# Fused linear attention and gated MLP on one core: the first chunk's k and r scaled on one engine, and two of four small norm steps of five chunks moved to another

## The chip, the cores and the metric

The kernel runs on one core of a Trainium2 chip. The metric is the device time of one execution in microseconds, the median of several runs; lower is better. The engines are named as in the profile: PE is the matrix engine (PEld its weight loads), DVE is VectorE, ACT is ScalarE, POOL is GpSimd, and SP is the queue that issues the transfers. Each works through its own list of instructions in order, and waits on the others through semaphores.

## The reference

Two stages follow one another. The first is a linear attention with a decaying state, over 4 batches, 8 heads, 768 steps and 48 channels per head:

```python
for t in range(S):
    cur = einsum('bhd,bhe->bhde', u * kt, vt)
    y[:, :, t] = einsum('bhd,bhde->bhe', rt, state + cur)
    state = w * state + einsum('bhd,bhe->bhde', kt, vt)
```

The second is a gated MLP on its output `x` (4 x 768 x 384):

```python
h = maximum(x @ w_in, 0)             # 1024 columns: u is the first half, v the second
v_n = (v - mean(v)) / sqrt(var(v) + 1e-6)
v_s = einsum('ts,bsd->btd', w_spatial, v_n) + b_spatial
out = (u * v_s) @ w_out
```

All of it is in float32; the large products are made of three passes over high and low parts of the operands.

## The kernel before, in words

The attention is done in 24 chunks of 128 time steps, 6 for each batch. For a chunk, `prep` (L588) multiplies k and r by powers of the decay (step "scale", L605), forms the products r·k·u (steps "rk", L609, and "rku", L610; for the first chunk "prod", L620, summed on PE, L627), scales another copy of k (step "ks", L615), sums (step "red", L632) and spreads the sums on a diagonal (step "dia", L635). `g1` (PE, L652 and L660) makes the scores and the state updates, `mid` masks and copies (L683 to L697), and `g2` (PE, L714) gives the chunk's part of `x`, which is split into high and low parts (steps "xh" on ACT and "xl" on DVE, L755).

For each chunk of x, `moe_v` (L768) then computes v (PE, L762 to L764) and normalizes it along the row. For the first five chunks ("early", `STA = 5`, all in batch 0) the row's sum and its sum of squares come from accumulating activations on ACT (L786, L790). Then follow, on columns of 128x1: the step "sqrt" on ACT (L797), the step "scales" on DVE, which is four instructions (L803 to L806), and the step "norm" on ACT (L815, L816). Columns of the small tile `q` are called `at(n)`: `at(7)` is the sum of squares, `at(9)` the root, and `at(12)` the factor that the norm multiplies by. The four steps of "scales" are one Newton step on the root and a reciprocal:

```python
e.tensor_scalar(out=p8(), in0=at(7), scalar1=part, scalar2=0.25 * EPS, op0=ALU.mult, op1=ALU.add)
e.reciprocal(out=at(10), in_=at(9))
e.tensor_scalar(out=p11(), in0=p8(), scalar1=at(10), scalar2=at(9), op0=ALU.mult, op1=ALU.add)
e.reciprocal(out=at(12), in_=p11())
```

In batch 0 the two intermediate columns `p8` and `p11` lie in PSUM (tile `cc`).

Two other steps matter below. `part` (L536) splits a loaded tile `wst` of the spatial weights into a high part on ACT and a low part on POOL (step "ws lo", L539); the 4 places of `wst` are taken again by the next loads when the low part is done. `from_f64` (L490) converts the other weights from double precision, mostly on DVE.

The order is not left to a scheduler of the compiler. A planner (`Plan`, L86) knows each step with the engines that it may run on and an estimated duration for each, simulates the engines, and chooses engine and start for every step. `issue` (L314) then writes the instructions in the order of the planned starts, and so fixes each engine's list. In that order, around the norms of the five early chunks, POOL's list and the DVE step that stands behind each "scales" are as follows ("sqrt" and "scales" mark only the places of these steps of ACT and DVE):

| chunk | POOL's list with the places of sqrt and scales | DVE's next step behind scales |
|---|---|---|
| 0 | rku, (sqrt 0), ws lo, (scales 0), rk, dia | red |
| 1 | rku, (sqrt 1), ws lo, ws lo, dia, rk, ws lo, (scales 1), rku, ws lo | first xl |
| 2 and 3 | (sqrt 2), rk, (sqrt 3), rku, (scales 2), ws lo, ws lo, ws lo, (scales 3), dia | 2: scale of k; 3: scale of r |
| 4 | dia, (sqrt 4), ab lo, (scales 4), ws lo, ws lo | red |

In the first chunk the planner put the scale of k on POOL and that of r on DVE, to start together; each reads two tiles in SBUF. "ab lo" (L825) is the low part of a normalized block of v.

Of the kernel before, what the change touches and what calls it, by code (L numbers as in the profile page):

```python
# [10 lines left out]
AF = mybir.ActivationFunctionType  # L11
ALU = mybir.AluOpType
# [14 lines left out]
ND = DH // P  # L27
TH = S // 2
EPS = 1e-6
GAIN, SHUN, HOLD = 2.0, 2.0, 40.0  # L30
SEEDS = ()
FIRST = """
# [53 lines left out]
class Plan:  # L86
# [6 lines left out]
    def op(self, eng, f, r=(), w=(), psum=(), dma=0, name="", after=(), port=None, n=0):  # L93
        o = Op()
        o.i, o.eng, o.f, o.preds, o.succ, o.bufs, o.new, o.dma = len(self.ops), eng, f, set(), [], [], [], dma
        o.n = n
        o.name, o.on, o.port = name, None, "P" in eng if port is None else port
        o.lag = 0.165 if "E" in eng else 0.0
        for x, write in [(x, False) for x in r] + [(x, True) for x in w] + [(x, True) for x in psum]:
            b, sub = x if isinstance(x, tuple) else (x, None)  # L100
            if o not in b.ops:
                if not b.ops and b.group:
                    o.new.append(b)
                b.ops.append(o)
                o.bufs.append(b)
            subs = list(b.state) if sub is None else [sub, None]
            for s in subs:
                if s in b.state:
                    last, readers = b.state[s]
                    if last is not None:  # L110
                        o.preds.add(last)
                    if write:
                        o.preds.update(readers)
            if write:
                if sub is None:
                    b.state = {None: (o, [])}
                else:
                    b.state[sub] = (o, [])
            else:
                for s in (list(b.state) if sub is None else [sub]):  # L120
                    b.state.setdefault(s, (b.state.get(None, (None, []))[0], []))[1].append(o)
                if sub is None and None not in b.state:
                    b.state[None] = (None, [o])
        o.preds.update(after)
        o.preds.discard(o)
        self.ops.append(o)
        return o
# [55 lines left out]
    def repeat(self, t0, seeds):  # L183
# [6 lines left out]
        if seeds:  # L190
            x, y = (sum(z) for z in zip(*(self.change(s) for s in seeds)))
            T = self.run(t0, x, y)
        return T

# [112 lines left out]
    def take(self, b, t):  # L307
# [3 lines left out]
        d.free.remove(x)  # L311
        b.slot = x[1]

    def issue(self, engines):  # L314
        for o in sorted(self.ops, key=lambda o: (o.start, o.i)):
            for b in o.new:
                b.tile = b.group.pool.tile(b.shape, b.dt, name=b.name, tag=b.slot, bufs=1)
            o.f(engines[o.on])


@with_exitstack
def fused_kernel(ctx, tc, rkT, rN, kN, vN, wT, uB, w_in, w_sp, b_sp, w_out, out):
    nc = tc.nc
# [6 lines left out]
    plan = Plan()  # L330
    op = plan.op
# [18 lines left out]
    def act(n):  # L350
        return (n + 185) / 1200
# [42 lines left out]
    eps = fixed([P, 1], "eps")  # L394
# [10 lines left out]
    q = lambda: tmp()[:, 0:256].rearrange("p (n c) -> p n c", n=NP)  # L405
# [32 lines left out]
    def raw_sp(s, t, i):  # L438
# [5 lines left out]
       name="warm")  # L444
# [5 lines left out]
    for p in range(NP):  # L450
        op({"V": 0.25}, lambda e, p=p: e.tensor_tensor_scan(
            out=q()[:, p, :], data0=wt()[:, p:p + 1].to_broadcast([P, 64]), data1=zz(), initial=1.0, op0=ALU.mult, op1=ALU.add),
           r=[wu, (tmp, "z")], w=[(tmp, "q", )], name="scan")
# [3 lines left out]
       w=[w128], name="w128")  # L457
    op({"P": 0.1}, lambda e: e.memset(uw(), 0.0), w=[(uw, j) for j in range(2)], name="memset")
    for j in range(2):
        op({"P": 0.25}, lambda e, j=j: e.tensor_tensor(  # L460
            out=uw()[64 * j:64 * j + 64, :, j], in0=wu()[64 * j:64 * j + 64, NP:2 * NP], in1=wu()[64 * j:64 * j + 64, 0:NP],
            op=ALU.mult), r=[wu], w=[(uw, j)], name="uw")
    op({"P": 0.3}, lambda e: e.tensor_tensor(out=diag(), in0=eye()[:, 0:64], in1=eye()[:, 64:P], op=ALU.add), r=[eye], w=[diag],
       name="diag")
    op({"P": 0.15}, lambda e: e.memset(mask(), 1.0), w=[mask], name="memset")
    for o, sign in ((64, 1), (0, -1)):
        op({"P": 0.3}, lambda e, sign=sign, o=o: e.affine_select(
            out=mask()[o:o + 64], in_=mask()[o:o + 64], pattern=[[-sign, 64]], compare_op=ALU.is_gt, fill=0.0, base=0,
# [299 lines left out]
    def moe_v(b, c):  # L768
        xh, xl = xs_all[b, c // 3]
        i, h = c % 3, c // 3  # L770
        o = slice(i * C, (i + 1) * C)
        pm = Buf(gM, [P, 512], F32, "pm")
        assert b * NC + c in there

        def f(e):
            for j in range(NK):
                mm3(e, pm(), xh()[:, j, o], xl()[:, j, o], wi[0][0]()[:, j], wi[0][1]()[:, j], j == 0, j == NK - 1)

        op({"E": 2.09}, f, n=18, r=[(x, (i, z)) for x in (xh, xl) for z in range(2 if b * NC + c < XPM else 1)] + wi[0], psum=[pm], name="v")
        if i == 0:  # L780
            vt[b, h] = Buf(gV, [P, 3, DH], F32, "v")
        vf, q = vt[b, h], Buf(gSM, [P, 16], F32, "q")
        at = lambda k: q()[:, k:k + 1]
        early = b * NC + c < STA
        if early:
            op({"A": act(DH) + 0.16}, lambda e: e.activation(out=vf()[:, i], in_=pm(), func=AF.Relu, accum_out=at(0)),  # L786
               w=[(vf, i), (q, 0)], psum=[pm], name="v")
            op({"A": 0.2}, lambda e: e.mul(at(6), at(0), -1.0 / DH), r=[(q, 0)], w=[(q, 6)], name="mean")
            junk = Buf(gF, [P, DH], mybir.dt.bfloat16, "junk", "j", 1)
            op({"A": sb(DH) + 0.3}, lambda e: e.activation(out=junk(), in_=vf()[:, i], func=AF.Square, bias=at(6), accum_out=at(7)),  # L790
               r=[(vf, i), (q, 6)], w=[junk, (q, 7)], name="square")
        else:
            acopy((vf, i), lambda: vf()[:, i], pm, lambda: pm(), DH, True, "v", {"V": vec(DH)}, AF.Relu)
            op({"V": 0.69}, lambda e: e.bn_stats(out=q()[:, 0:6], in_=vf()[:, i]), r=[(vf, i)], w=[(q, 0)], name="stats")
            op({"V": 0.18}, lambda e: e.bn_aggr(out=q()[:, 6:8], in_=q()[:, 0:6]), r=[(q, 0)], w=[(q, 6), (q, 7)], name="aggr")
        part = 0.25 / DH if early else 0.25
        op({"A": 0.2}, lambda e: e.activation(out=at(9), in_=at(7), func=AF.Sqrt, bias=eps(), scale=part), r=[(q, 7), eps],  # L797
           w=[(q, 9)], name="sqrt")
        o8 = DM + HC + 2 * ((b * NC + c) % 8)
        p8, p11 = (lambda: at(8), lambda: at(11)) if b else (lambda: cp()[:, o8:o8 + 1], lambda: cp()[:, o8 + 1:o8 + 2])  # L800

        def scales(e):
            e.tensor_scalar(out=p8(), in0=at(7), scalar1=part, scalar2=0.25 * EPS, op0=ALU.mult, op1=ALU.add)  # L803
            e.reciprocal(out=at(10), in_=at(9))
            e.tensor_scalar(out=p11(), in0=p8(), scalar1=at(10), scalar2=at(9), op0=ALU.mult, op1=ALU.add)
            e.reciprocal(out=at(12), in_=p11())  # L806
            if not early:
                e.tensor_scalar(out=at(13), in0=at(6), scalar1=at(12), scalar2=-1.0, op0=ALU.mult, op1=ALU.mult)  # L808

        op({"V": 0.65 if early else 0.81}, scales, r=[(q, 6), (q, 7), (q, 9)], w=[(q, 10)] + ([] if b else [(cc, ("q", o8))]), name="scales", port=not early)  # L810

        def norm(e):
            x = vf()[:, i]
            if early:
                e.mul(at(13), at(6), at(12))  # L815
            e.activation(out=x, in_=x, func=AF.Identity, bias=at(13), scale=at(12))  # L816

        op({"A": 1.01 if early else 0.81}, norm, r=[(q, 10), (q, 6)], w=[(vf, i)], name="norm")
# [81 lines left out]
    def late(b, t, d):  # L900
        pm = Buf(gM, [P, 512], F32, "pm")
        xh, xl = xs_all[b, t]
        x = xsum[b, t, d]
        assert {b * NC + 3 * t + x for x in range(3)} <= there
        uv = lambda: pm()[:, 0:TH]

        def f(e):
            for j in range(NK):
                mm3(e, uv(), wi[1][0]()[:, j, blk[d]], wi[1][1]()[:, j, blk[d]], xh()[:, j], xl()[:, j], j == 0, j == NK - 1)

        op({"E": 1.6}, f, n=18, r=[xh, xl, *wi[1]], psum=[pm], name="u")
        op({"V": vec(TH)}, lambda e: e.scalar_tensor_tensor(out=uv(), in0=uv(), scalar=0.0, in1=x(), op0=ALU.max, op1=ALU.mult),  # L912
           r=[x], psum=[pm], name="gate")
        gt = gs[b, t, d] = Buf(gAB, [P, 2, TH], F32R, "gt")
        acopy((gt, 0), lambda: gt()[:, 0], pm, uv, TH, True, "gt hi")
        op({"V": vec(TH)}, lambda e: e.tensor_tensor(out=gt()[:, 1], in0=uv(), in1=gt()[:, 0].bitcast(F32), op=ALU.subtract),
           r=[(gt, 0)], w=[(gt, 1)], psum=[pm], name="gt lo")
# [157 lines left out]
    for b in range(B):  # L1075
# [3 lines left out]
        o = [(lambda b=b, t=t, i=i: moe_out(b, t, i)) for t in range(2) for i in range(3)]  # L1079
        dr = [lambda b=b: (s3(b), direct(b, 0))]  # L1080
        if b:
# [4 lines left out]
            A = [Step(m) for m in range(6 * b, 6 * b + 10)]  # L1086
# [13 lines left out]
    for f in seq:  # L1100
        f()
    T = plan.repeat(14.0, SEEDS)
    plan.issue({"E": nc.tensor, "A": nc.scalar, "V": nc.vector, "P": nc.gpsimd, "S": nc.sync})


# [53 lines left out]
```

## Time and profile before

| what | value |
|---|---|
| median of 3 runs | 345.95 us (344.8 to 346.01) |
| profiled execution, its own time | 346.39 us |
| span in its profile | 344.7 us |
| busy: PE, DVE, ACT, POOL | 326.5, 258.0, 155.9, 198.1 us |
| PE instructions (matmuls) | 5414 |
| data moved | 43.87 MB in 26263 packets |

The span is the time from the first to the last instruction of the profiled execution; about 1.7 us lie around it. Starts in the rows are counted from the start of the span. A row of the timeline has the start, the duration, the engine, the line of the kernel, the operation, the tiles it writes and reads, and in brackets the time for which the engine was idle before it and what ended that. A row of the chain of waits has the start, the duration and the work that the end of the program is traced back to at that time. A row of the stretches has, for each engine, its busy time and (x) its instructions within that stretch.

### The profile page before, as it was taken

The page shows a single profiled execution, that of the slowest core. Times are in us where ns is not written, and L with a number is a line of the kernel's source. Part 1 is how long each engine was busy: PE and PEld are TensorE (multiplying, and loading weights), DVE is VectorE, ACT ScalarE, POOL GpSimd, SP SyncE. Part 2 cuts the span into 40 slices and gives each one's busy share as a digit, 9 for nine tenths or more (in the row PEclk, how much of TensorE's full clock was granted, in tenths as well). Part 3 has the DMA queues.
Part 4 walks back from the last instruction along what each step waited for, and adds up shares of the span by engine and source line. Part 5 has one row for each costly group of instructions (what it writes and reads, how often), then busy time and mean ns, then how long its engine had stood idle before and what let it go on. Part 6 is the DMA issues. An engine that isn't in the chain of part 4 may idle for free.

```text
span 344.7 us, 12648 instructions
## 1 busy us (share of the span) xinstructions
PE 326.5 (95%) x5414; PEld 297.5 (86%) x5414; DVE 258.0 (75%) x567; ACT 155.9 (45%) x372; POOL 198.1 (57%) x193
## 2 busy tenths in 40 slices
PE   2887798999999999999999999999999999999996
PEld 2665687899999898999899888999998799999995
DVE  6897799898989878899887688688476575674520
ACT  5433899832453547614413555623043546331121
POOL 5767586654799969989955154989052020840000
PEclk9999999999999999999999999999999999999999
DMA  7989588653513735514423253414041000100012
GB/s 235 387 235 327 169 256 298 199 174 114 193 60 104 226 120 164 172 39 142 139 63 104 74 175 103 151 60 142 0 126 55 28 25 34 59 0 0 3 46 91
DMA packets 26263, 43.87 MB, mean 127 GB/s; under 512 B 3040, under 2 KB 15328, under 8 KB 26208
## 3 DMA queue, kind: packets, MB, share of 16 engines
q1 hardware_dynamic: 26208, 43.07, 39.2%
q8 instruction: 42, 0.69, 0.9%
q14 instruction: 13, 0.11, 0.1%
HBM read 38.34 MB, written 4.72 MB: 125 GB/s over the span
## 4 chain that ended last, share of the span: by engine, by line
PE 83%; DMA 4%; POOL 4%; issue 3%; DVE 2%; ACT 2%; SPq 1%; DVEq 0%; POOLq 0%
PE pm L945 20%; PE pm L762 16%; PE pm L764 15%; PE pm L763 15%; PE xp L714 8%; PE ps L652 4%; PE ps L660 3%; DMA wst<-w_sp 2%; DMA kn<-kN 1%; POOL ws L539 1%; PE pm L714 1%; PE pm L520 1%; SPq L363 1%; POOL rn L609 1%; POOL rn L610 1%
## 5 line engine op out<-in xcount | busy, mean ns | idle before, releaser
L945 PE MATMUL pm<-wst,ab 128*128 128x384 f32 x216 | 41.2, 339 | 0.5 <-issue 0.5
L376 ACT CAST gt<-pm 128x384 fp32r<-128x384 f32 x26 | 12.4, 480 | 60.4 <-DVE pm L912 57.6
L825 POOL TENSOR_TENSOR ab<-v,ab 128x384 fp32r<-128x384 f32 x22 | 23.8, 1093 | 26.4 <-ACT ab L376 26.4
L945 PEld LDWEIGHTS pm<-wst,ab 128*128 128x128 f32 x216 | 37.7, 188 | 0.8 <-issue 0.6
L762 PE MATMUL pm<-xh,wiuh 128*128 128x384 f32 x96 | 32.9, 343 | 0.0
L762 PE MATMUL pm<-woh,gt 128*128 128x384 f32 x96 | 32.9, 343 | 0.0
L764 PE MATMUL pm<-woh,gt 128*128 128x384 f32 x96 | 32.5, 338 | 0.3 <-issue 0.3
L764 PE MATMUL pm<-xh,wiul 128*128 128x384 f32 x96 | 32.4, 337 | 0.0
L763 PE MATMUL pm<-wol,gt 128*128 128x384 f32 x96 | 32.3, 337 | 0.0
L763 PE MATMUL pm<-xl,wiuh 128*128 128x384 f32 x96 | 32.3, 337 | 0.0
L945 PE MATMUL pm<-ws,ab 128*128 128x384 f32 x162 | 31.5, 338 | 0.0
L635 POOL TENSOR_TENSOR a<-diag,dg 128x512 f32<-128x512 f32 x17 | 17.9, 1053 | 23.1 <-PE xp L714 8.9
L762 PE MATMUL pm<-wivh,xh 128*128 128x512 f32 x72 | 29.2, 406 | 1.0 <-ACT wiuh L376 1.0
L376 ACT COPY sb<-t 64x192 f32<-64x192 f32 x48 | 16.8, 350 | 27.3 <-DVE t L690 26.7
L945 PEld LDWEIGHTS pm<-ws,ab 128*128 128x128 f32 x162 | 28.6, 188 | 0.1
L764 PE MATMUL pm<-wivh,xl 128*128 128x512 f32 x72 | 28.5, 396 | 0.0
L763 PE MATMUL pm<-wivl,xh 128*128 128x512 f32 x72 | 28.5, 395 | 0.0
L609 POOL TENSOR_TENSOR rn<-rn,kn 128x384 f32<-128x384 f32 x16 | 17.5, 1091 | 15.1 <-DMA kn<-kN 8.2
L610 POOL TENSOR_TENSOR rn<-rn,ub 128x384 f32<-128x384 f32 x21 | 23.2, 1106 | 4.9 <-DVE rn L609 3.8
L957 DVE TENSOR_TENSOR tp<-pm,tp 128x384 f32<-128x384 f32 x30 | 16.6, 553 | 10.4 <-PE pm L945 10.1
L816 ACT ACTIVATE v<-v,q 128x512 f32<-128x512 f32 x24 | 19.5, 815 | 7.5 <-DVE q L808 7.1
L683 DVE COPY_PREDICATED a<-mask,ps 128x512 f32<-128x512 uint32 x24 | 17.8, 742 | 6.5 <-PE ps L660 6.3
(169 smaller groups left out, 876.4 us busy)
## 6 DMA issues: line engine op xcount, KB each, us to landing
kT<-rkT SPq DMA_DIRECT2D x24, 256.0 KB, 3.7
rT<-rkT SPq DMA_DIRECT2D x24, 256.0 KB, 3.5
vn<-vN SPq DMA_DIRECT2D x24, 256.0 KB, 4.1
kn<-kN SPq DMA_DIRECT2D x24, 200.0 KB, 3.4
wst<-w_sp SPq DMA_DIRECT2D x24, 192.0 KB, 4.2
out<-ob SPq DMA_DIRECT2D x24, 192.0 KB, 1.9
rn<-rN SPq DMA_DIRECT2D x23, 192.0 KB, 3.0
raw<-w_in SPq DMA_DIRECT2D x8, 384.0 KB, 5.1
```

The costliest lines, as they stand in the source:

```text
L376: e.activation(out=o_f(), in_=i_f(), func=func) if func else e.copy(o_f(), i_f())
L609: op(VP, lambda e: e.tensor_tensor(out=rn()[:, 0:DM], in0=rn()[:, 0:DM], in1=kn()[:, 0:DM], op=ALU.mult), r=[kn], w=[rn], name="rk")
L610: op(VP, lambda e: e.tensor_tensor(out=rn()[:, 0:DM], in0=rn()[:, 0:DM], in1=ub(), op=ALU.mult), r=[ub], w=[rn], name="rku")
L635: op({"V": vec(512) + 0.05, "P": 1.06}, lambda e: e.tensor_tensor(out=a().rearrange("s j p t -> s (j p) t"), in0=(diagp() if e is nc.vecto ...
L683: op({"V": 0.74}, lambda e: e.copy_predicated(out=a(), mask=mask().bitcast(U32).unsqueeze(1).unsqueeze(1).to_broadcast([P, 2, NP, HC]), da ...
L714: e.matmul(x[z][32 * g:32 * g + 32, jt * HC:(jt + 1) * HC], lhsT, rhs, start=(z, g) not in began, stop=True, skip_group_check=True, tile_p ...
L762: e.matmul(o, lh, rh, start=first, stop=False)
L763: e.matmul(o, lh, rl, start=False, stop=False)
L764: e.matmul(o, ll, rh, start=False, stop=last)
L816: e.activation(out=x, in_=x, func=AF.Identity, bias=at(13), scale=at(12))
L825: op(VP, lambda e: e.tensor_tensor(out=t()[:, 1], in0=src(), in1=t()[:, 0].bitcast(F32), op=ALU.subtract), r=[(t, 0), src_b], w=[(t, 1)], ...
L945: e.matmul(pm(), a()[:, x, i], w()[:, y, i], start=not began and i + q_ == 0, stop=i + q_ == 4, skip_group_check=True)
```

## The change

The step "sqrt" of an early chunk now also issues, on POOL, the first of the four scale steps (`at(8)` from `at(7)`). "scales" issues the first reciprocal on DVE, then the second `tensor_scalar` (`at(11)`) on POOL, and hands the last reciprocal to `issue`, which writes it on DVE right behind the next DVE step, or ahead of the first step that depends on "scales", whichever comes first. The intermediate columns lie in the SBUF tile `q`. The planner knows nothing of it: its costs and its order are the same. After planning, every "scale" step that was planned to start before 7 us is put on DVE; these are k and r of the first chunk, of which r was there already. `DEBUG` is never set.

```diff
+    rest = None
     def issue(self, engines):
+        left = None
         for o in sorted(self.ops, key=lambda o: (o.start, o.i)):
 ...
+            if self.rest and left in o.preds:
+                self.rest()
+                self.rest = None
+            late = self.rest
             o.f(engines[o.on])
+            if late and o.on == "V":
+                late()
+                self.rest = None if self.rest is late else self.rest
+            if self.rest and self.rest is not late:
+                left = o
 ...
-        op({"A": 0.2}, lambda e: e.activation(out=at(9), in_=at(7), func=AF.Sqrt, bias=eps(), scale=part), r=[(q, 7), eps],
-           w=[(q, 9)], name="sqrt")
+        def root(e):
+            e.activation(out=at(9), in_=at(7), func=AF.Sqrt, bias=eps(), scale=part)
+            if early:
+                nc.gpsimd.tensor_scalar(out=at(8), in0=at(7), scalar1=part, scalar2=0.25 * EPS, op0=ALU.mult, op1=ALU.add)
+        op({"A": 0.2}, root, r=[(q, 7), eps], w=[(q, 9)], name="sqrt")
 ...
         def scales(e):
+            if early:
+                e.reciprocal(out=at(10), in_=at(9))
+                nc.gpsimd.tensor_scalar(out=at(11), in0=at(8), scalar1=at(10), scalar2=at(9), op0=ALU.mult, op1=ALU.add)
+                plan.rest = lambda: e.reciprocal(out=at(12), in_=at(11))
+                return
 ...
     T = plan.repeat(14.0, SEEDS)
+    for o in plan.ops:
+        if o.name == "scale" and o.start < 7:
+            o.on = "V"
     plan.issue({"E": nc.tensor, "A": nc.scalar, "V": nc.vector, "P": nc.gpsimd, "S": nc.sync})
```

More of the change, by code (lines that the diff above doesn't have):

```diff
@@ L29 @@
 EPS = 1e-6
+DEBUG = None
 GAIN, SHUN, HOLD = 2.0, 2.0, 40.0
@@ L1102, in fused_kernel @@
     T = plan.repeat(14.0, SEEDS)
+    if DEBUG:
+        DEBUG(plan, T)
+    for o in plan.ops:
+        if o.name == "scale" and o.start < 7:
+            o.on = "V"
     plan.issue({"E": nc.tensor, "A": nc.scalar, "V": nc.vector, "P": nc.gpsimd, "S": nc.sync})
```

## The prediction

> **What bounds the kernel now.** I read the busy times at the head of the page first, then the table of stretches, then what PE waited for, and only then the timeline where the edited steps stand.
>
> ```profile
> PE 326.5 (95%) x5414; PEld 297.5 (86%) x5414; DVE 258.0 (75%) x567; ACT 155.9 (45%) x372; POOL 198.1 (57%) x193
> ...
> 36.00:46.00 10.00, 9.20 (x206) 7.22 (x206) 8.78 (x23) 8.48 (x25) 5.97 (x7) 1.00 0.62 174
> 46.00:56.00 10.00, 9.18 (x293) 7.23 (x291) 9.58 (x27) 9.11 (x28) 7.21 (x8) 1.00 0.86 276
> 56.00:66.00 10.00, 9.84 (x110) 9.15 (x111) 8.89 (x28) 8.83 (x23) 6.67 (x7) 1.00 0.82 262
> 66.00:80.00 14.00, 13.83 (x320) 12.59 (x318) 12.80 (x25) 6.55 (x17) 8.66 (x9) 1.00 0.46 148
> 80.00:120.00 40.00, 40.00 (x743) 36.53 (x740) 35.61 (x74) 19.22 (x45) 33.74 (x34) 1.00 0.47 142
> ```
>
> PE (the number behind each stretch's length) is full from about 68 us on. So what delays PE before that is not made good later: a shift there arrives at the end almost whole. Before 68 us PE has gaps, and DVE in the stretch from 46 to 56 is busy for 9.58 of 10 us. All edits stand before 65 us. What PE waited for in that time is this (us in total, times, longest):
>
> ```profile
> PE pm L714 <- issue: 2.8, 2, 2.0
> PE ps L660 <- issue: 2.2, 2, 1.2
> PE pm L762 <- ACT wiuh L376: 1.0, 1, 1.0
> PE ps L652 <- DVE rT L605: 0.9, 1, 0.9
> PE xp L714 <- ACT sb L376: 0.2, 1, 0.2
> ```
>
> The largest, 2.8 and 2.2 us, are ascribed to no engine ("issue"), so no edit of POOL or DVE reaches them. The 0.9 us before L652 is the first chunk's scale, which is edited. The last row, 0.2 us, is the last gap before PE is full: there ACT, not PE, sets the pace.
>
> **The first chunk's scales.** One DVE step is added, one POOL step removed.
>
> ```profile
> 5.27 1.27 POOL L605 TENSOR_TENSOR kT<-kT,tt 128x512 f32<-128x512 f32 x1 [1.43 <-DVE w L456]
> 5.33 1.75 DVE L605 TENSOR_TENSOR rT<-rT,tt 128x512 f32<-128x512 f32 x1 [0.19 <-DVE w L456]
> ...
> 6.79 0.59 ACT L1019 COPY cc<-tt 128x512 f32<-128x512 f32 x1
> 7.20 0.98 PEld L652 LDWEIGHTS ps<-rT,kT 64*64 64x64 f32 x32 [1.24 <-POOL kT L605]
> ...
> 7.42 0.55 DVE L615 TENSOR_TENSOR kn<-kn,cc 128x384 f32<-128x384 f32 x1 [0.33 <-ACT cc L1019]
> ...
> 8.04 0.98 PEld L660 LDWEIGHTS ps<-vn,kn 64*64 64x64 f32 x32
> ...
> L601 DVE TENSOR_TENSOR kT<-kT,tt x8: 692/1094/1383, 114.0 to 256.5; 128x512 f32<-128x512 f32 x8
> ```
>
> Beside POOL's scale, DVE's took 1.75 us and ended at 7.08. The same operation on the same kind of tiles has a minimum of 0.69 us (last row, min/median/max); I take that, since POOL then has nothing to run until its "prod" step, which itself needs both scales. Two of them on DVE end at 5.33 + 2 x 0.69 = 6.71, 0.37 us sooner, and L652 starts so much sooner. But PE's next group, L660, needs kn from L615. That started at 7.42, with DVE free since 7.08, because it waited for ACT's L1019 (6.79 + 0.59 = 7.38), which the edit does not touch. So kn is still ready at 7.42 + 0.55 = 7.97, and L660's weights were loaded from 8.04. The sooner start ends in a gap between L652 and L660. I take 0; the end of the range is a gain of 0.4 us, if L615's wait is put down to the wrong step.
>
> **The norm's steps, what is saved.** Per early chunk DVE loses the two `tensor_scalar` steps.
>
> ```profile
> 53.60 1.01 POOL L609 TENSOR_TENSOR rn<-rn,kn 128x384 f32<-128x384 f32 x1 [2.70 <-DMA kn<-kN]
> ...
> 54.43 0.15 DVE L803 TENSOR_SCALAR cc<-q 128x1 f32<-128x1 f32 x1
> ...
> 54.68 0.28 DVE L805 TENSOR_SCALAR cc<-cc,q 128x1 f32<-128x1 f32 x1
> 54.69 1.00 POOL L610 TENSOR_TENSOR rn<-rn,ub 128x384 f32<-128x384 f32 x1
> 54.99 0.17 DVE L806 RECIPROCAL q<-cc 128x1 f32<-128x1 f32 x1
> 55.08 0.67 DVE L605 TENSOR_TENSOR kT<-kT,cc 128x512 f32<-128x512 f32 x1
> 55.65 3.01 POOL L539 TENSOR_TENSOR ws<-wst,ws 128x384 fp32r<-128x384 f32 x3
> 55.66 0.61 DVE L755 TENSOR_TENSOR xl<-pm,xh 128x192 fp32r<-128x192 f32 x2
> ...
> 56.47 0.19 PEld L764 LDWEIGHTS pm<-wivh,xl 128*128 128x128 f32 x1
> ...
> 56.68 1.31 SPq L363 DMA_DIRECT2D wst<-w_sp  x2
> ```
>
> The four steps take 55.08 - 54.43 = 0.65 us of DVE. Two reciprocals remain, like L806 0.17 us each, so 0.31 us are saved per chunk, 1.6 us over five. That is worth something only where DVE is what PE waits for, and none of PE's waits above names a DVE step but L605 of the first chunk. I count the saving at nothing.
>
> **The norm's steps, what is added.** Each chunk adds two POOL steps of one column, and DVE's last reciprocal now waits for POOL with all of DVE queued behind it. The nearest rows for such a POOL step are the smallest ones it runs:
>
> ```profile
> L460 POOL TENSOR_TENSOR uw<-wu x2: 196/230/263, 2.5 to 2.7; 64x4 f32<-64x4 f32 x2
> ```
>
> No row has a POOL `tensor_scalar`. On DVE, the second one (with two columns as scalars) took 0.28 against 0.15 us for the first. I take 0.25 us for each of the two POOL steps, nearest to L460; the ends are 0.1 (part hidden behind the step before) and 1.0 us (the full POOL step of L610, 128x384). The Trainium skill, in "GPSIMD Engine Reference", section 4.1 "Engine selection", advises VectorE for elementwise work because GpSimd is about twice as slow on two-input operations. By that rule, twice DVE's 0.15 and 0.28 us would give 0.86 us for the pair instead of my 0.5, an estimate; no row here decides it.
>
> Where it counts is decided by the order of POOL's list. I go through the chunks with what covered POOL:
>
> ```profile
> POOL ws L539 <- ACT ws L376: 3.7, 2, 3.3
> POOL rn L609 <- DMA kn<-kN: 3.4, 2, 2.7
> POOL ab L825 <- ACT ab L376: 3.4, 2, 1.7
> ...
> POOL wst L539 <- ACT wst L376: 1.3, 1, 1.3
> ```
>
> - Chunk 0: the first step falls into the 3.3 us wait before "ws lo". The second delays "rk" and "rku" by 0.25 us, and the 1.3 us wait before the next "ws lo" takes that up. Cost 0.
> - Chunk 1: the first step falls into that 1.3 us. The second pushes "rku" and a "ws lo", and the 2.7 us wait of "rk" for its kn load follows. The DVE reciprocal waits some 0.1 us for POOL. Cost 0.
> - Chunks 2 and 3 have no cover. POOL runs L609, (first step of chunk 3), L610, (second step of chunk 2), then three "ws lo" without a gap: 53.60, 54.69, 55.65. With 0.25 us in each place the "ws lo" steps begin at 56.15 instead of 55.65. The wait is on DVE too: chunk 2's last reciprocal stands behind the scale of k (done near 55.3) and waits for a POOL step that ends at 55.65 + 0.5 = 56.15. DVE is stopped for 0.85 us, and "xl" starts near 56.4 instead of 55.66. PE's first weight load of xl, at 56.47, needs both halves, done at 56.4 + 0.61 = 57.0: PE loses 0.5 us there.
> - Chunk 3's second step stands behind the third "ws lo", and chunk 4's behind "ab lo". Both hold DVE again (about 0.5 us more in chunk 3), but "ab lo" had 1.7 us of cover, and DVE then stood idle until ACT's root of chunk 5 anyway:
>
> ```profile
> DVE q L804 <- ACT q L797: 0.6, 1, 0.6
> ```
>
> So chunks 3 and 4 add nothing to the 0.5 us.
>
> How the 0.5 us of POOL goes on is shown by the chain of waits:
>
> ```profile
> 55.65 2.00 POOL ws L539 x2
> ...
> 57.67 4.62 DMA wst<-w_sp
> ...
> 62.31 0.03 ACT ws L376
> ...
> 67.77 1.33 PE xp L714 x77
> ```
>
> SP issues the two `wst` loads (56.68) as the "ws lo" steps free their places; the second lands at 62.29 and ACT, which starts with it at 62.31, has its list full from there until it releases PE at 67.77, where PE had waited 0.2 us. So POOL's 0.5 us becomes ACT's and then PE's, from 67.77 to 68.27. PE's own loss of 0.5 us at 56.47 arrives at the same place and runs beside it; the two do not add.
>
> **The sum.** 0 (first chunk) + 0 (saved DVE) + 0.5 (chunk 2 and 3) = +0.5 us. Against the profiled execution's 346.39 us that is 346.9; the median of the runs stands 0.44 us lower, so 346.4. Bounds: 345.95 - 0.4 + 0.2 = 345.75 with both unknowns at their good ends, 345.95 + 2 x 1.0 = 347.95 with POOL's steps at their dear end. The runs before reach from 344.8 to 346.01, so about 0.5%, 1.7 us, is what a measurement of this kernel can tell from no change.
>
> **The rivals.**
>
> - Nothing arrives (346.0 and a little below): POOL's steps overlap the steps around them, or the first chunk's 0.4 us does reach L627. For it: POOL's independent steps start up to 0.04 us before the one ahead has ended (54.69 + 1.00 against 55.65). Against it: DVE's stop at 55.3 needs only the order, not a dear step.
> - Slower, by POOL's price: place, the pair behind L609 and L610; price, as much as a full POOL step each, 2.0 us, so 347.95. It decides above 1.73 us for the pair, 0.87 each. Against it: L460's 0.23 us. For it: no row shows the operation, and it reads columns as scalars.
> - Faster, by DVE: if what PE, ACT and POOL wait for from 36 to 68 us is at bottom DVE's load, the saved 1.6 us count. All of PE's gaps in the four stretches from 36 to 80 us are 0.80 + 0.82 + 0.16 + 0.17 = 1.95 us, so 344.0 at the utmost, and a clear gain needs nearly all of it. Against it: the waits name "issue" and ACT.
> - The step in PE's speed moves:
>
> ```profile
> 20.66 1.09 PE L521 MATMUL pm<-lw,neg 128*128 128x384 f32 x1
> ...
> 22.52 0.63 PE L521 MATMUL pm<-lw,neg 128*128 128x384 f32 x1
> ```
>
> The same matmul took 1.09 and then 0.63 us, with the granted clock given as 1.00 in both. Each us by which this step moves, after a sooner L652 and a longer gap behind it, is worth 1 - 0.63 / 1.09 = 0.42 us either way; beyond 1.73 us it would have to move by 4.1 us. The Trainium skill, "TensorE: Matmul & The Clock Gate", Part 1, has the clock double after a free-running window of about 3.4 us of activity; one window would be 1.4 us here, an estimate, and no run here shows what times it.
>
> **How the numbers follow.** Forecast 0.55, nothing arrives 0.22, POOL's price 0.13 (two thirds of it past 0.5%), DVE's gain 0.06, the step in speed 0.04 (half each way). With the spread of the runs, the forecast's own range is 345.6 to 347.3. For 8 in 10 the range takes in most of POOL's price and some of the gain: 345.0 to 347.9. Faster by over 0.5%: 0.09; slower: 0.14; within: 0.77.
>
> **What would show it.** L605 twice on DVE from 5.33 at about 0.69 us each, L652 near 6.8 and L660 still near 8.0. Two POOL rows of 128x1 per early chunk, near 0.25 us. A DVE wait of 0.8 us or so for POOL before chunk 2's last reciprocal, xl near 56.4, the first "ws lo" near 56.15, PE's L714 near 68.3. I am wrong if L660 starts well before 8.0, if the small POOL rows take over 0.5 us, or if PE's sum before 68 us moves by more than 1 us either way.

## The result and the profile after

The change came out slower by half a percent at first and by a quarter in a second timing. The ratio of the changed kernel's runs to those of before is 1.0051 with a 95% interval of 1.0031 to 1.0071 (medians 347.68 and 345.64 us, some 19 executions each), or +1.8 us (+1.1 to +2.5). A second timing of the same kernel gave 1.0023 (0.9994 to 1.0051), +0.8 us. The forecast was +0.5 us, 346.4, with a range of 345.0 to 347.9. All differences in us below are ratios times 346 us. The first profiled execution of the changed kernel and that of chunk 3 alone (below) ran at mean granted clocks of 0.759 and 0.588 and are not used; the profile shown is that of the second timing. Its lines 605, 609, 615, 714, 755, 762 and 815 of before have become 619, 623, 629, 728, 769, 776 and 839.

The page of the changed kernel, head:

```profile
span 343.2 us, 12646 instructions
PE 325.4 (95%) x5414; PEld 296.6 (86%) x5414; DVE 257.9 (75%) x558; ACT 156.1 (45%) x372; POOL 199.7 (58%) x202
```

DVE has 9 instructions fewer and POOL 9 more: the ten small steps moved, and one scale went the other way. This one execution has a shorter span than the profiled one of before (344.7), so single spans say nothing here; a difference has to be read inside the execution, between two places that both kernels have.

The first chunk, in the timeline:

```profile
5.39 0.69 DVE L619 TENSOR_TENSOR kT<-kT,tt 128x512 f32<-128x512 f32 x1 [0.19 <-DVE w L470]
6.00 0.69 DVE L619 TENSOR_TENSOR rT<-rT,tt 128x512 f32<-128x512 f32 x1
6.74 0.94 PEld L666 LDWEIGHTS ps<-rT,kT 64*64 64x64 f32 x32 [0.72 <-DVE rT L619]
...
7.48 0.55 DVE L629 TENSOR_TENSOR kn<-kn,cc 128x384 f32<-128x384 f32 x1 [0.79 <-ACT cc L1043]
8.09 0.94 PEld L674 LDWEIGHTS ps<-vn,kn 64*64 64x64 f32 x32 [0.40 <-DVE kn L629]
```

The step is as forecast: 0.69 us each, PE's first group 0.46 us sooner, and its second group at 8.09 against 8.04, because L629 still waits for ACT. The 0.46 us have become a gap of 0.40.

The small POOL steps (times in ns, min/median/max):

```profile
L815 POOL TENSOR_SCALAR q<-q x5: 190/190/191, 35.5 to 58.9; 128x1 f32<-128x1 f32 x5
L824 POOL TENSOR_SCALAR q<-q x5: 331/345/347, 38.3 to 61.2; 128x1 f32<-128x1 f32 x5
```

0.19 and 0.35 us: 0.54 for the pair, against 0.5 in the forecast. Around chunk 2 the timeline of the changed kernel is:

```profile
51.90 1.00 POOL L623 TENSOR_TENSOR rn<-rn,kn 128x384 f32<-128x384 f32 x1 [1.75 <-DMA kn<-kN]
...
52.06 0.93 PE L728 MATMUL pm<-rT,sb 128*32 128x64 f32 x48
...
52.98 0.19 POOL L815 TENSOR_SCALAR q<-q 128x1 f32<-128x1 f32 x1
...
53.26 1.00 POOL L624 TENSOR_TENSOR rn<-rn,ub 128x384 f32<-128x384 f32 x1
...
54.24 0.34 POOL L824 TENSOR_SCALAR q<-q 128x1 f32<-128x1 f32 x1
...
54.62 0.16 DVE L825 RECIPROCAL q<-q 128x1 f32<-128x1 f32 x1 [0.80 <-POOL q L824]
54.70 0.60 DVE L769 TENSOR_TENSOR xl<-pm,xh 128x192 fp32r<-128x192 f32 x2
...
55.15 0.19 PEld L776 LDWEIGHTS pm<-wivh,xh 128*128 128x128 f32 x1 [1.64 <-ACT q L839]
```

DVE is stopped for 0.80 us ahead of chunk 2's last reciprocal, xl stands behind it, and PE's v group behind xl. The chain of waits of the same stretch now runs through the moved steps, from a load to PE:

```profile
48.05 3.71 DMA kn<-kN
51.90 1.00 POOL rn L623
52.98 0.20 POOL q L815
...
54.24 0.35 POOL q L824
54.62 0.17 DVE q L825
54.82 0.30 ACT q L839
55.18 0.47 PE pm L776
```

In the chain before, this place held a load of `wst` and the ws lo steps; POOL's L609 of 53.60 us and its kn load were not in it.

### The profile page after: what moved, and what is told of

Same layout as the page of the kernel before. It is cut to its first block, busy times and chain, and to the rows that moved or that the text cites. A ratio compares the mean times of both kernels' runs of the same rounds, so it can differ in the third digit from the quotient of the medians.

```text
span 399.4 us, 12646 instructions
## 1 busy us (share of the span) xinstructions
PE 384.2 (96%) x5414; PEld 328.3 (82%) x5414; DVE 257.2 (64%) x558; ACT 155.8 (39%) x372; POOL 196.0 (49%) x202
## 4 chain that ended last, share of the span: by engine, by line
PE 94%; DMA 1%; issue 1%; POOL 1%; SPq 1%; ACT 1%; DVE 0%; DVEq 0%; ACTq 0%; POOLq 0%
PE pm L969 20%; PE pm L776 19%; PE pm L778 18%; PE pm L777 18%; PE xp L728 7%; PE ps L666 4%; PE ps L674 3%; PE pm L728 3%; DMA rn<-rN 1%; PE pm L534 1%; SPq L377 1%; ACT sb L390 0%; POOL kT L619 0%; POOL rT L619 0%; PE pm L535 0%
## 5 line engine op out<-in xcount | busy, mean ns | idle before, releaser
L969 PE MATMUL pm<-wst,ab 128*128 128x384 f32 x216 | 49.3, 392 | 0.0
L969 PEld LDWEIGHTS pm<-wst,ab 128*128 128x128 f32 x216 | 42.7, 204 | 2.9
L969 PE MATMUL pm<-ws,ab 128*128 128x384 f32 x162 | 37.7, 390 | 0.0
L776 PE MATMUL pm<-woh,gt 128*128 128x384 f32 x96 | 37.3, 389 | 0.0
L776 PE MATMUL pm<-xh,wiuh 128*128 128x384 f32 x96 | 37.2, 387 | 0.0
L778 PE MATMUL pm<-woh,gt 128*128 128x384 f32 x96 | 37.0, 385 | 0.0
L777 PE MATMUL pm<-wol,gt 128*128 128x384 f32 x96 | 37.0, 385 | 0.0
L778 PE MATMUL pm<-xh,wiul 128*128 128x384 f32 x96 | 36.8, 383 | 0.0
L777 PE MATMUL pm<-xl,wiuh 128*128 128x384 f32 x96 | 36.7, 382 | 0.0
L776 PE MATMUL pm<-wivh,xh 128*128 128x512 f32 x72 | 34.5, 479 | 1.0 <-ACT wiuh L390 1.0
L778 PE MATMUL pm<-wivh,xl 128*128 128x512 f32 x72 | 33.1, 460 | 0.0
L624 POOL TENSOR_TENSOR rn<-rn,ub 128x384 f32<-128x384 f32 x21 | 23.1, 1099 | 6.1 <-DVE rn L623 5.0
L936 DVE SCALAR_TENSOR_TENSOR pm<-pm,tp 128x384 f32<-128x384 f32 x26 | 14.7, 566 | 17.3 <-PE pm L778 17.3
L623 POOL TENSOR_TENSOR rn<-rn,kn 128x384 f32<-128x384 f32 x16 | 16.5, 1029 | 17.3 <-PE pm L778 5.6
```

The source lines that it names most:

```text
L623: op(VP, lambda e: e.tensor_tensor(out=rn()[:, 0:DM], in0=rn()[:, 0:DM], in1=kn()[:, 0:DM], op=ALU.mult), r=[kn], w=[rn], name="rk")
L624: op(VP, lambda e: e.tensor_tensor(out=rn()[:, 0:DM], in0=rn()[:, 0:DM], in1=ub(), op=ALU.mult), r=[ub], w=[rn], name="rku")
L776: e.matmul(o, lh, rh, start=first, stop=False)
L777: e.matmul(o, lh, rl, start=False, stop=False)
L778: e.matmul(o, ll, rh, start=False, stop=last)
L969: e.matmul(pm(), a()[:, x, i], w()[:, y, i], start=not began and i + q_ == 0, stop=i + q_ == 4, skip_group_check=True)
```

## The experiments

Below, "timed" is the ratio to the kernel before on the same chip, with its 95% interval. The theories as they stood at first: A, the pair of small steps of chunks 2 and 3 is the whole loss; B, the first chunk's scales cost it; C, it is scatter; D, each of the five chunks costs its share.

**The change again** (no edit):

> The changed kernel once more, for a profile at full granted clock and a second timing. Theory A (the pair of small GpSimd steps behind L623 and L624, chunks 2 and 3, holds VectorE and the ws lo steps): 0.5 to 2 us above before; GpSimd's small steps about 0.2 and 0.34 us; VectorE stopped 1 to 1.5 us before chunk 2's last reciprocal; the three ws lo steps 0.5 us or more later than before's 55.65, and the last gap of PE near 68 us as much later. Theory B (the first chunk's two scales on VectorE cost it): PE already late before 50 us. Theory C (no cause in the edits, runs scatter): 0 +- 0.7 us.

Timed 1.0023 (0.9994 to 1.0051), the profile shown above. The small steps are as expected by A; the stop, 0.80 us, is shorter than the 1 to 1.5 expected. Counted from L623 (L609 before), the ws lo steps begin at 2.64 us against 2.05 and PE's xp at 14.77 against 14.17, both later by what A says; counted from the start of the span they are sooner, since this execution was ahead there already (L728 at 52.06, L714 before at 53.56).

**Only the first chunk's scales** (timed twice):

```diff
-            if early:
+            if early and c < 0:          # in root and in scales
```

> Only the first chunk's k and r are both on VectorE; the norm's steps as before. Theory A: 0 to -0.4 us against before (345.6 or a little less); PE's second group L674 of the first chunk starts near 8.0 as before. Theory B: +1 us or more, most of the change's loss.

> e2_scales_only once more, to add to its timing: k and r of the first chunk both on VectorE, the norm as before. My prediction's step: 0 to -0.4 us. If e2's -0.8 us was more than scatter, -0.5 to -1 us again.

Timed 0.9977 (0.9954 to 1.0001) and 1.0023 (0.9997 to 1.0049): -0.8 and +0.8 us for one and the same kernel, on two occasions. Together they are zero, as the profiles say (L674 at 8.1). B is out as the cause of a loss of 1.8 us. The pair also shows what these intervals are worth: two timings of one kernel lie 1.6 us apart, so no single difference under about 1 us is trusted below. Every later kernel was timed on one occasion only.

**Only the norm's steps**:

```diff
-        if o.name == "scale" and o.start < 7:
+        if False and o.name == "scale" and o.start < 7:
```

> Only the norm's steps are moved, in all five chunks; the first chunk's k is scaled on GpSimd as before. Theory A: the change's whole loss, +0.5 to +2 us. Theory B: 0 +- 0.5 us.

Timed 1.0076 (1.0044 to 1.0107), +2.6 us. The loss sits in the norm's steps.

**Only chunks 0, 1 and 4, and only chunks 2 and 3** (both without the scales' edit):

```diff
-            if early:
+            if early and c not in (2, 3):     # the other kernel: c in (2, 3)
```

> Only the norm's steps are moved, and only in chunks 0, 1 and 4; chunks 2 and 3 have all four on VectorE. Theory A: 0 +- 0.5 us, since each of these places has cover; no stop of VectorE over 0.5 us. Rival D (each of the five chunks costs its share, through ACT or VectorE): three fifths of e3's loss, about +1 us.

> Only the norm's steps are moved, and only in chunks 2 and 3. Counted from the start of L623 (the rk step ahead of the two), the ws lo steps start at 2.65 us instead of before's 2.05, and PE's xp L728 at 14.65 to 14.8 instead of 14.17. Theory A (these two chunks are the whole loss): +0.5 us by that count, and as much as e3_norm_only in time, +1 to +2.6 us. Rival D (each chunk its share): two fifths of e3's +2.6, +1.0 us, the rest being e4's +0.8.

Timed 1.0022 (0.9991 to 1.0052) for chunks 0, 1 and 4 and 1.0045 (1.0019 to 1.0071) for chunks 2 and 3, +0.8 and +1.6 us. Only the second is clear of zero; by the times alone, A and D are not parted. The stops of DVE in chunks 0, 1 and 4 are 0.6 us at most, a little over the 0.5 expected. The profile of chunks 2 and 3 parts them better, since it shows the stop at 1.72 us and PE waiting 2.6:

```profile
53.61 0.93 PE L728 MATMUL pm<-rT,sb 128*32 128x64 f32 x48
...
54.50 1.01 POOL L623 TENSOR_TENSOR rn<-rn,kn 128x384 f32<-128x384 f32 x1 [1.87 <-DMA kn<-kN]
...
57.23 0.16 DVE L825 RECIPROCAL q<-q 128x1 f32<-128x1 f32 x1 [1.72 <-POOL q L824]
57.31 0.60 DVE L769 TENSOR_TENSOR xl<-pm,xh 128x192 fp32r<-128x192 f32 x2
...
57.76 0.19 PEld L776 LDWEIGHTS pm<-wivh,xh 128*128 128x128 f32 x1 [2.69 <-ACT q L839]
...
69.16 0.54 PE L728 MATMUL xp<-rT,sb 128*32 128x64 f32 x24
```

Here the kn load ended later against PE (L623 0.89 us after PE's L728, not 0.16 us ahead of it as in the changed kernel's profile), and the stop grew by as much. Counted from L623, the ws lo steps (2.65 us) and PE's xp (14.66) are as expected. That the kn load's lateness now reaches PE was not in my theory.

**Four times the POOL steps in chunks 2 and 3**:

```diff
-            if early:
+            for _ in range(4 if early and c in (2, 3) else 0):
                 nc.gpsimd.tensor_scalar(out=at(8), ...)
 ...
-            if early:
+            if early and c in (2, 3):
 ...
+                for _ in range(4):
                     nc.gpsimd.tensor_scalar(out=at(11), ...)
```

> As e5_norm_23, with each of the four small GpSimd steps of chunks 2 and 3 issued four times over (the same result written again). The pair behind L623 and L624 was 0.19 + 0.34 us, about 0.6 with the gaps; three more of each is +1.6 to +1.8 us. Theory A: the ws lo steps at 4.3 us or more behind L623, PE's xp 1.6 us or more later than in e5, and the time 1.5 to 2 us above e5's. Theory C (runs scatter, GpSimd's delay hidden): time as e5's.

Timed 1.0154 (1.0106 to 1.0203), +5.3 us, 3.7 above the kernel with single steps and not the 1.5 to 2 expected. The direction is A's, the size is not. Its timeline and its table of stretches (PE's busy time behind the length, the granted clock third from the end):

```profile
59.14 0.16 DVE L826 RECIPROCAL q<-q 128x1 f32<-128x1 f32 x1 [4.52 <-POOL q L825]
...
59.71 0.77 PE L776 MATMUL pm<-wivh,xh 128*128 128x512 f32 x1 [5.08 <-ACT q L840]
```

```profile
54.60:59.70 5.10, 0.03 (x2) 0.02 (x1) 0.58 (x4) 1.25 (x5) 4.40 (x11) 0.89 0.59 209
59.70:62.00 2.30, 2.29 (x6) 1.82 (x7) 2.17 (x6) 2.23 (x6) 2.30 (x4) 0.50 0.32 85
62.00:64.00 2.00, 2.00 (x6) 1.62 (x5) 0.31 (x2) 0.62 (x3) 1.70 (x5) 0.50 0.57 147
64.00:68.00 4.00, 4.00 (x21) 4.00 (x21) 2.58 (x8) 2.71 (x7) 2.44 (x3) 0.82 0.57 177
```

PE stood still for 5.1 us, and then its granted clock is 0.50 from 59.7 to about 65.4 (0.82 in the last stretch is 1.4 of its 4 us at 0.50). That is a second loss on top of the wait: from L776's weight load to PE's xp it takes 14.00 us here and 11.40 in the kernel with single steps, 2.6 us more. The way from PE's L728 to L776 is longer by 2.5 us (6.67 against 4.15). Both together are more than the 3.7 us timed; this profile is of one of the two longest of the six executions (353.09 us, the other 353.33, the rest 349.15 to 350.56). So the half clock accounts for the direction of the miss, and the exact sum is open.

**POOL's copies only**: all four steps on DVE as before, the two POOL steps of chunks 2 and 3 issued in addition.

```diff
-            if early:
+            if early and c in (2, 3):     # the first small step, in root
 ...
+            if early and c in (2, 3):
+                nc.gpsimd.tensor_scalar(out=at(14), in0=at(8), scalar1=at(10), scalar2=at(9), op0=ALU.mult, op1=ALU.add)
             e.tensor_scalar(out=p11(), in0=p8(), scalar1=at(10), scalar2=at(9), op0=ALU.mult, op1=ALU.add)
```

> All four steps of every norm stay on VectorE as before; in chunks 2 and 3 GpSimd runs the two small steps in addition, at the places that the change gives them, their results unused. So the ws lo steps are late as in e5 but VectorE is never stopped. If GpSimd's lateness carries the loss: xp 0.5 us late from L623, time as e5's. If VectorE's stop carries it: xp as before, time 0 +- 0.4 us against before.

Timed 1.0018 (0.9988 to 1.0048), +0.6 us. PE's wait at L776 is 1.2 us, as with chunks 0, 1 and 4 moved (before 1.0). Inside the profile (L728 at 52.12, xp at 66.61) it is 14.49 us from PE's L728 to xp, 0.28 more than before's 14.21:

```profile
51.59 0.56 DVE L515 TENSOR_SCALAR pm<-hb 128x384 uint32<-128x384 uint32 x1
...
52.12 0.93 PE L728 MATMUL pm<-rT,sb 128*32 128x64 f32 x48
...
54.49 0.61 DVE L769 TENSOR_TENSOR xl<-pm,xh 128x192 fp32r<-128x192 f32 x2
...
54.96 0.19 PEld L776 LDWEIGHTS pm<-wivh,xh 128*128 128x128 f32 x1 [1.38 <-ACT q L838]
...
55.53 2.98 POOL L553 TENSOR_TENSOR ws<-wst,ws 128x384 fp32r<-128x384 f32 x3
```

But that 0.28 us is no cost of POOL's. PE's L728 started 0.27 us sooner against DVE's list here, 0.53 us behind the start of L515, where L714 started 0.80 behind that of L501. xl follows L515 after 2.90 us, as it follows L501 before, and from L776's weight load to xp it is 11.65 us against 11.64. The three ws lo steps began 0.57 us behind that weight load; before, they began 0.48 us ahead of it. So POOL's lateness alone cost nothing in this execution, and the loss of chunks 2 and 3 needs DVE's stop.

**Chunk 3 alone and chunk 2 alone** (both without the scales' edit):

```diff
-            if early:
+            if early and c == 3:              # the other kernel: c == 2
```

> Only chunk 3's norm steps are moved. By now the theory is E: chunk 2's last reciprocal waits on VectorE for a GpSimd step that stands behind L623 and L624, whose kn load lands when it lands; xl stands behind it, and PE's v group L776 starts 0.46 us after xl's start. Theory E: no stop of VectorE ahead of xl, PE's wait at L776 1.0 to 1.4 us as in before and e4, time 0 to +0.4 us (the first step still holds the ws lo steps by 0.27 us). Rival F (GpSimd's lateness and later stops cost as much): half of e5's +1.55 us or more.

> Only chunk 2's norm steps are moved. Theory E: VectorE stopped 0.8 to 1.7 us before the reciprocal, PE's wait at L776 1.5 to 2.6 us, and nearly e5's loss, +1.0 to +1.6 us. Rival F: half of e5's or less, +0.7 us.

Timed 1.0014 (0.9991 to 1.0037) and 1.0009 (0.9982 to 1.0037). The first, +0.5 us (-0.3 to +1.3), is as expected within its interval. The second misses: I expected +1.0 to +1.6 us and measured +0.3 (-0.6 to +1.3). Its stop was only 0.68 us and PE's wait 1.2. Two things explain the profile: without chunk 3's first step between L623 and L624 the queue ahead is 0.26 us shorter (53.38 to 54.48, that is 1.10 us, against 1.36 in the changed kernel), and L623 started 0.18 us before PE's L728 in that execution. So chunk 2's stop is the place, but chunk 3's step lengthens it, and neither alone makes the loss.

**The whole change, with rku behind chunk 2's second step**:

```diff
+    for o in plan.ops:
+        if o.name == "rku" and 52 < o.start < 52.6:
+            o.start += 0.4
```

> The whole change, with one GpSimd step moved: the rku step (L624) that stood ahead of chunk 2's second small step now stands behind it. GpSimd is as late as before for the ws lo steps, but VectorE waits for one long step less. Theory E: the stop before chunk 2's reciprocal falls by about 1.0 us, to 0 to 0.7 us, PE's wait at L776 to 1.0 to 1.5 us, and the time to +0.3 to +0.8 us against before. Rival F: as the change, +1.2 to +1.8 us.

Timed 1.0012 (0.9986 to 1.0039), +0.4 us. The stop before chunk 2's reciprocal is gone. One of 1.35 us before chunk 3's remains, and the stretch from L728 to xp is nevertheless the shortest of all (table below), so chunk 3's stop costs nothing in it. By the time alone this kernel is not clearly parted from the change (+1.8 and +0.8 us). What PE waits for at L776 is now named differently:

```profile
PE pm L776 <- DVE xl L769: 0.9, 1, 0.9
```

In its timeline the weight load starts 0.47 us behind xl, and ahead of the end of ACT's "wiuh" (55.04 + 0.50), which was named before:

```profile
54.97 0.62 DVE L769 TENSOR_TENSOR xl<-pm,xh 128x192 fp32r<-128x192 f32 x2
55.04 0.50 ACT L390 CAST wiuh<-pm 128x384 fp32r<-128x384 f32 x1
...
55.44 0.19 PEld L776 LDWEIGHTS pm<-wivh,xh 128*128 128x128 f32 x1 [1.01 <-ACT xh L390]
```

**The whole change, with the second step back on DVE**:

```diff
-                nc.gpsimd.tensor_scalar(out=at(11), in0=at(8), ...)
-                plan.rest = lambda: e.reciprocal(out=at(12), in_=at(11))
+                e.tensor_scalar(out=at(11), in0=at(8), ...)
+                e.reciprocal(out=at(12), in_=at(11))
```

> The whole change, but the second small step stays on VectorE, with the last reciprocal right behind it; only the first step runs on GpSimd, for all five chunks. Theory E: VectorE waits only for a step that is long done (chunk 2's stands ahead of L623), no stop over 0.3 us, PE's wait at L776 1.0 to 1.3 us, time 0 +- 0.5 us against before. Rival F: a third to a half of the change's loss, +0.5 to +0.9 us.

Timed 0.9989 (0.9962 to 1.0016), -0.4 us: no difference from before, and 2.2 and 1.2 us below the change's two timings; the first of these differences is clear of their intervals, the second is not. No stop of DVE, and PE's wait is 1.0 us.

**All profiles side by side.** Each number is a difference of starts, from rows like those above, within one execution: L623 (L609 before) counted from PE's L728 (L714), DVE's stop ahead of chunk 2's reciprocal, and the stretch from that L728 to PE's xp, behind which PE is full. The rows of before for it:

```profile
52.76 0.56 DVE L501 TENSOR_SCALAR pm<-hb 128x384 uint32<-128x384 uint32 x1
...
53.56 0.93 PE L714 MATMUL pm<-rT,sb 128*32 128x64 f32 x48
...
56.13 0.19 PEld L762 LDWEIGHTS pm<-wivh,xh 128*128 128x128 f32 x1 [1.11 <-ACT wiuh L376]
...
67.77 0.54 PE L714 MATMUL xp<-rT,sb 128*32 128x64 f32 x24 [0.17 <-ACT sb L376]
```

| kernel | L623 from L728, us | DVE stopped, us | L728 to xp, us |
|---|---|---|---|
| before | +0.04 | 0 | 14.21 |
| scales only, twice | +0.40, +0.65 | 0 | 14.36, 13.98 |
| chunks 0, 1, 4 | +0.02 | 0 | 14.24 |
| POOL's copies only | +0.76 | 0 | 14.49 |
| first step only | +0.28 | 0 | 13.98 |
| rku behind | -0.05 | 0 | 13.86 |
| chunk 2 alone | -0.18 | 0.68 | 14.22 |
| the change | -0.16 | 0.80 | 14.61 |
| norm only | +0.27 | 1.39 | 14.92 |
| chunks 2 and 3 | +0.89 | 1.72 | 15.55 |

In the upper six rows, a late L623 costs nothing that can be seen: at +0.65 the stretch is 13.98. Their scatter, 13.86 to 14.49, is what a single row can be trusted to; some 0.3 us of it is where L728 falls against DVE's list. In the last three, which have both steps of chunks 2 and 3, the stretch grows with L623's lateness, by 0.94 us for 1.05 us. That is the coupling: VectorE now stands behind GpSimd's queue, whose head waits for a load. Behind the stop the way is the same: from L776's weight load to xp it is 11.39 to 11.41 us in seven of the twelve profiles, the kernels with norm only and with chunks 2 and 3 among them, 11.52 in the change and 11.64 before. The kn load was landing at different times against PE from one execution to the next already before; it did no harm then.

## Why the prediction was right or wrong

- First chunk, 0: right in mechanism and size. PE's second group loads at 8.09, kn still waits for ACT, and two timings average to nothing.
- POOL's price, 0.25 us each: right as a sum, 0.19 + 0.35 us. The rival by POOL's price is out. Twice DVE's duration, 0.86 us for the pair, did not come: it was 0.19 against DVE's 0.15, and 0.35 against 0.28. The Trainium skill ("GPSIMD Engine Reference", section 4.1 "Engine selection") states the factor of two for two-input operations and puts one-input operations at roughly line rate; these steps have one input column, with constants or two more columns as scalars, so it is the second that bears on them, and the forecast worked with the first.
- Saved DVE, counted at nothing: with the first step alone moved and no stop (the last kernel), the time is that of before, but the reason that I gave does not hold. I took from the waits that PE waited for ACT ahead of its v group. In twelve profiles, all that are used here, L776's weight load starts 0.45 to 0.47 us after xl's start (55.66 and 56.13 before, 57.31 and 57.76 with chunks 2 and 3), whatever ACT does. With rku moved it starts while ACT's "wiuh" still runs, and there the profile itself names DVE's xl (its rows stand with that kernel). So by this lag the 1.0 us in the row "PE pm L762 <- ACT wiuh" ended with DVE's xl, and whatever moves xl there moves PE. I had PE losing only from its third weight load on. A saving of DVE reaches PE by the same way. From DVE's L515 (L501 before) to xl it takes 2.90 us before and 2.49 with rku behind, where nothing stops DVE. In the last four rows of the table it takes 3.16, 3.28, 3.87 and 4.21 us, and each of these is 2.90 less 0.42 plus the stop, to 0.01 us. So the moved steps save 0.42 us at this place, and a stop costs only what it exceeds that by. The saving comes with the second step: with the first alone moved it is 2.90 again. Even without a stop the time shows no gain (+0.4 us, -0.5 to +1.3).
- Chunks 0, 1 and 4, cost 0: not contradicted. The stretch is 14.24 against 14.21, and the time +0.8 us with an interval that holds zero.
- Chunks 2 and 3, +0.5 us: right in place and order, mis-sized. This is the term of the sum that came out too small. Counted from the start of L609 the working holds: it has xl 2.80 us behind it (53.60 and 56.4), and xl stands 2.80, 2.80 and 2.81 us behind L623 in the change, with norm only, and with chunks 2 and 3. But I took L609's start, and so DVE's stop of 0.85 us, from one execution, in which it happened to lie 0.04 us after PE's L714. Measured stops are 0.80, 1.39 and 1.72 us, and the stretch to xp is longer by 0.40, 0.71 and 1.34 us, as the kn load lands. And an xl that comes 0.74 us late (56.4 for 55.66) holds PE up for 0.74 us and not 0.5, by the lag above. That the one profile of the change lies near the 0.5 us (+0.40) is luck: L623 came 0.36 us sooner against DVE's list than in the execution I had worked from (0.48 us behind L515, 0.84 behind L501 before), which offset it. The timed loss was +1.8 and +0.8 us for the change, +2.6 for its norm part and +1.6 for chunks 2 and 3. The forecast named the wait on POOL and DVE's queue behind it, but not that L609's own wait for kn, which I had counted as cover in chunk 1, stands at the head of that queue.
- "The two do not add", with POOL's 0.5 us going through the ws lo steps, the load and ACT to PE: this path carried nothing that was seen. The copies put the ws lo steps over 1 us later against PE's v group than before, and PE's xp stood where it was (11.65 and 11.64 us behind the group). What arrived is PE's own wait alone.
- The rival by the step in PE's speed: the step does move, but as far as these single executions show not through the edit: the same matmul took 0.63 us already at 20.21 us in the changed kernel (20.66 us: 1.09 before), at 20.28 and 19.67 with chunks 0, 1 and 4 and with the copies, whose first chunk is as before, and still 1.09 at 22.46 and 22.82 with the scales only and at 22.64 and 23.00 with norm only and chunks 2 and 3. So it scatters by some 3 us from one execution to the next, with and without the scales' edit; at the forecast's 0.42 us for each that is about 1.2 us, an estimate. It stands far ahead of L728 and does not touch the stretch in the table, but it may be one reason why spans and single times scatter. PE's waits at L776 of 1.5 to 2.6 us, in the changed kernel and its parts, left the granted clock at 1.00.

Open: the profiles show 0.4 to 1.3 us, each for one execution, while the norm part alone timed at 1.5 to 3.7 us, above the whole change (+0.8) timed on the same occasion. The record has a hint. A mean granted clock of 0.995 over an execution is what one stretch of 3.4 us at 0.50 leaves (3.4 x 0.5 of 344 us). Among the executions that the ratios use, the mean clock is below 0.998 in 28 of 98 of the kernel before, timed beside the experiments, and these are 1.0 us longer than its others. With both steps of chunks 2 and 3 moved and rku ahead (the change twice, norm only, chunks 2 and 3) it is 34 of 50; with the other edits, the four-fold one left out, 29 of 92. For norm only it is 8 of 10: those 8 average 348.8 us, the other two 346.4, and its profile is one of the two. So a part of the timed loss goes with executions in which PE runs a stretch at half clock. Where in them it lies, and whether the stop starts it, no trace here shows. Something in chunks 0, 1 and 4 (+0.8 us, not clear of zero) is not excluded either.

## What to carry to other kernels

When a step is moved to another engine and its result comes back, look at what the helper's queue holds ahead of it at that place, and above all whether a load is waited for there: the engine that was relieved now inherits that wait, with its scatter. Size such a stop not from one execution but over the spread of the load's landing, and set what the relieved engine saves at that place against it. And check a wait's named releaser against a fixed lag in several places: the engine that starts a constant time before, whatever the others do, is the likelier releaser.

## What the runs showed of the hardware that I had not expected

After PE had stood idle for 5.1 us, it worked at a granted clock of 0.50 for 5.7 us and its first 128x512 matmul took 0.77 us instead of 0.47; after 2.6 us idle, with chunks 2 and 3 moved, the clock was 1.00:

```profile
55.00:57.70 2.70, 0.23 (x23) 0.07 (x8) 0.98 (x4) 1.45 (x5) 2.53 (x5) 1.00 0.85 281
57.70:62.00 4.30, 4.21 (x21) 3.82 (x22) 3.73 (x10) 4.17 (x11) 3.74 (x5) 1.00 0.78 251
```

The Trainium skill ("TensorE: Matmul & The Clock Gate", Part 1) states half clock after an idle window of about 3.4 us; these two stops agree with it. Four other profiles do not, if the window is taken as one gap. With the scales only, PE's longest gap there was 0.98 us, and its granted clock was 0.50 from 30.7 to 34.1; before, a gap of 2.02 us at the same place left it at 1.00. The first three rows are of the scales only, the others of before:

```profile
30.37 1.01 PE L728 MATMUL pm<-a,vn 64*32 64x64 f32 x58 [0.98 <-issue]
31.32 0.79 PE L776 MATMUL pm<-wivh,xh 128*128 128x512 f32 x1
31.91 0.63 PE L777 MATMUL pm<-wivl,xh 128*128 128x512 f32 x1
```

```profile
30.84 0.81 PE L714 MATMUL pm<-a,vn 64*32 64x64 f32 x59 [2.02 <-issue]
31.59 0.50 PE L762 MATMUL pm<-wivh,xh 128*128 128x512 f32 x1
31.92 0.39 PE L763 MATMUL pm<-wivl,xh 128*128 128x512 f32 x1
```

The other three drops to 0.50 came after gaps of 1.20 and 1.81 us near 31 us (chunks 2 and 3, the copies) and 1.92 us near 40 us (chunk 2 alone). Each of the four lasted 3.4 us. So the length of the last gap does not settle it here.

A one-column `tensor_scalar` on GpSimd took 0.19 us with constants and 0.35 us with two columns as scalars, nearly what DVE needs (0.15 and 0.28).
